# Clustered attention and gated convolution: routing by VectorE block transposes, with the order of every queue written out

## The chip, the cores and the metric

The kernel runs on one core of a Trainium2 chip. That core has TensorE (PE: matrix products and transposes by matrix product, from SBUF into PSUM), VectorE (DVE), ScalarE (ACT), GpSimd (POOL) and SyncE (SP, here only an issuer of DMAs), and 16 DMA engines. Each engine takes its own queue of instructions strictly in order; an instruction waits until the semaphores that it names have been raised. The metric is the device time of one execution in microseconds (us), lower is better. Where a time of a part is given, it comes from one profiled execution.

## The reference, cut to what matters

Two parts follow each other. The first is attention in which a query sees a key only if both fall to the same cluster, one of 16 per head:

```
B, H, S, D = 4, 8, 768, 64;  16 clusters per head
q_assign = argmax over c of  q_n . c_n        (q_n, c_n: divided by their norms; k_assign alike)
mask     = q_assign[:, :, :, None] == k_assign[:, :, None, :]
scores   = where(mask, q k^T / sqrt(D), -1e9);  attn = softmax(scores)
x        = attn v, heads side by side          -> (4, 768, 512)
```

The second is a gate around a circular convolution of length 768, done by Fourier transform:

```
x1, x2, x3 = x @ w_proj                        (512 -> 3 x 512)
y   = x1 * irfft(rfft(x2) * rfft(filter)) * x3
out = y @ w_out                                -> (4, 768, 512), fp32
```

## The kernel before

**The work.** Four batches times two groups of four heads make eight groups n = 0 to 7 (`NG`), and each group has two head pairs pr = 0, 1. For each group there is a `routing` step (L544), which prepares queries, keys and the mask, and for each pair an `attention` step (L647). After every second group, a batch's x is complete and `hyena` (L800) does projection, transform, gate and output of that batch, among the attention work of later groups; the last batch's comes after all attention.

**Attention.** For each of six key tiles of 128 keys, three score products per pair (L664) fill a PSUM bank each with 512 columns. ScalarE takes the exponential of each (L678, L681) into an SBUF tile `p`. A p-by-v block of eight matmuls (`pv`, L688, the instructions at L692) adds into two PSUM banks (4 and 5). The denominators are sums of `p` over key tiles in `acc`: the first two tiles are added in three pieces, on VectorE or GpSimd (L709), the other four by VectorE whole (L713). The sums over partitions then go by accumulating DMAs from POOL's queue (L746) and through DRAM (L750, L752), or for some groups by PE (L726).

**The mask.** It is no separate operation: 16 rows below the 64 (or above, for the second head) of the bf16 operands `aug` of the score product hold one-hot words of the cluster, 0 or 1 on the key side and -BIG or 0 on the query side, with BIG = 262144, so that a score of another cluster falls by BIG before the exponential.

**Routing, groups 1 to 7.** PE transposes queries and keys (`tr2`, L562; `tr` for group 1). Casts write the 64 rows of `aug` (L581). Then the clusters:

1. `sim` (L592, instructions at L595): 16 matmuls of 32 rows by 384 give similarities, 128 rows (query or key, pair, head, cluster) by 768 tokens, in two PSUM banks.
2. Two copies of them to SBUF by ScalarE or VectorE (L600, executed in the helper at L265 or L267).
3. `simT` (L606, at L608): six fp32 128x128 transposes on PE, into two more PSUM banks. Now 128 tokens lie on the partitions and 48 groups of 16 clusters in a row.
4. VectorE: the largest of 16 (L616, in two halves), the comparison with it (L618, two halves), a product with falling numbers BIG*16 to BIG*1 (`revx`, L621) to settle ties, four steps of maxima (`largest`, L629), and one last step on keys (is_equal) and on queries (subtract), L633.
5. One DMA transpose from SP's queue (L638) brings the words `oh` back to rows, 128 x 768 in `ohT`.
6. Eight DMAs (`masks`, L469) put 16 rows each into the `aug` tiles. A mask's 16 rows lie four apart in `ohT`.

Group 0 goes another way (`first_masks`, L474), which the change leaves as it is but for its place in the order.

**What sets the order.** Each step registers operations with `Plan.op` (L85): engines it may run on, an assumed duration, a due time, what it reads and writes, and the PSUM banks that it takes. `Plan.place` (L114) is a list scheduler that runs when the program is built. It takes at each step an engine, an operation and free banks by readiness and due time, shifted for each operation by a table `NUDGE`, with a table `ONLY` that fixes the engine for some. What it returns is the order of all queues, and the bank of every product. Loads are held back to a short time before they are due (`LEAD`).

**Shapes of PE's array.** `array` (L50) gives each PE operation the shape in which it drives the array: 32, 64 or 128 columns wide. Scores, projections and inverse transforms take the shape of the operation before them, and `product` (L70) issues them in halves of 64 or whole (L75, L73).

**VectorE and GpSimd.** Operations marked `lock` on GpSimd are made to wait for the last locked one of VectorE that stands before them in the order (L1164).

Of the kernel before, what the change touches and what calls it, by code (L numbers as in the profile page):

```python
# [35 lines left out]
LEAD = 2.99901  # L36
FIRST = 2
BUSY = 8.09741
HELD = 4
# [3 lines left out]
THIRDS = [[(0, 0, 512)], [(0, 512, 768), (1, 0, 256)], [(1, 256, 768)]]  # L43
HOLD = {"score": "score", "o": "o"}
AFTER = {"PE": .16}
OVERLAP = {"ACT": .09, "DVE": .08}
MODES = {"pv": 64, "bc": 64, "half": 64, "sim": 32, "den": 32, "score": 0, "proj": 0, "inv": 0}


# [28 lines left out]
class Plan:  # L78

    def __init__(self):
        self.ops, self.writers, self.reads = [], {}, {}

    def op(self, eng, fn, due, r=(), w=(), alloc=None, free=(), lock=False, byts=0, after=(), kind=None, lat=0.0):  # L85
        o = Op()
        o.eng = eng if isinstance(eng, dict) else {eng[0]: eng[1]}
        o.fn, o.due, o.alloc, o.free, o.lock, o.byts, o.kind = fn, due, alloc, free, lock, byts, kind
        o.seq = len(self.ops)
        o.due += NUDGE.get(o.seq, 0.0)  # L90
# [23 lines left out]
    def place(self, free0, banks_for, switch=0.1, wait=0.1, rate=215e3, bonus=10.84378, margin=0.02195, shape=1.63806):  # L114
        free = dict(free0)
        bank_free = [0.0] * 8
        ready = {e: [] for e in free}
        pend = 0
        st = SimpleNamespace(pool=0.0, dve=0.0, bw={}, last=None, kind=None, score=0, o=0, tail=0,
                             held=dict(score=0, fill=0, o=0))  # L120
# [3 lines left out]
        def enqueue(o):  # L124
# [4 lines left out]
            for e in o.eng:  # L129
                ready[e].append(o)  # L130
# [1068 lines left out]
```

## Time and profile before

| | |
|---|---|
| runs | 385.18, 386.62, 389.62 us (median 386.62) |
| span of the profiled execution, first to last instruction | 383.4 us |
| PE busy | 366.2 us, 96% |
| VectorE busy | 335.8 us, 88% |
| ScalarE busy | 258.7 us, 67% |
| GpSimd busy | 115.3 us, 30% |
| granted TensorE clock, mean | 0.997 |
| PE's first matmul | 6.27 us, held by the first load of queries |
| data moved by DMA | 47.19 MB, mean 123 GB/s |

How to read it: the profile is of one execution, and the span leaves out what lies around the first and last instruction; the median of the runs is 3.2 us above the span. A row of a group has the line of the kernel, the engine, the operation, what it writes and reads, the shape and the number of times, then the busy time in us and the mean length of one in ns, then the idle time of that engine just before, and what ended that idle time. PEld is the loading of weights, which goes beside matmuls. A row of stages has the stretch and its length, the busy time of each engine in the order PE, PEld, VectorE, ScalarE, GpSimd with the number of instructions, then the granted clock, the share of the DMA engines and GB/s. A mean over the whole span mixes a start (to 24 us), a middle and a tail (from 340 us), and each has limits of its own.

### The profile page before, as it was taken

Reading aid. Unit: us, or ns where it says so; the run is one execution under the profiler, and the core shown is the slowest. Engines: PE = TensorE matmul, PEld = TensorE weight load, DVE = VectorE, ACT = ScalarE, POOL = GpSimd, SP = SyncE. Lnnn points to the kernel's source line nnn. Section 1 sums busy time; section 2 is a strip of 40 time slices with the busy share of each in tenths; the row PEclk is TensorE's granted clock in tenths of the full one; section 3 lists DMA queues with packets and bytes.
Section 4 is the critical chain, followed back from the end, with each engine's and each line's share of the span. In section 5 each row is a group of like instructions: output and inputs, shape, how many; then the busy total and the mean of one; then the engine's idle time right before and its main releaser. Section 6 shows DMA issues by size and latency. Waiting matters only on the chain.

```text
span 383.4 us, 8667 instructions
## 1 busy us (share of the span) xinstructions
PE 366.2 (96%) x3337; PEld 223.0 (58%) x3343; DVE 335.8 (88%) x497; ACT 258.7 (67%) x483; POOL 115.3 (30%) x155
## 2 busy tenths in 40 slices
PE   3999997999999999999999999999999899999995
PEld 2555454445455564655465665667578566557883
DVE  8778797888899689988999997998998899999982
ACT  5998878787885986588784656877762458712142
POOL 8522302011014454322342443222330452212500
PEclk9999999999999999999999999999999999999998
DMA  9909967642688678466986888854666641200124
GB/s 174 237 21 208 192 151 153 149 96 78 138 164 163 111 145 143 97 114 105 194 132 163 124 166 212 131 77 77 105 97 162 146 68 9 78 11 2 55 113 164
DMA packets 93861, 47.19 MB, mean 123 GB/s; under 512 B 82088, under 2 KB 87676, under 8 KB 93820
## 3 DMA queue, kind: packets, MB, share of 16 engines
q1 hardware_dynamic: 87836, 36.84, 43.3%
q0 software_dynamic: 2704, 8.98, 16.3%
q10 hardware_dynamic: 3280, 0.82, 1.2%
q8 instruction: 26, 0.43, 0.5%
q14 instruction: 15, 0.12, 0.1%
HBM read 31.59 MB, written 7.40 MB: 102 GB/s over the span
## 4 chain that ended last, share of the span: by engine, by line
PE 73%; DVE 17%; ACT 4%; issue 3%; POOL 1%; DVEq 0%; POOLq 0%; ACTq 0%
PE bank L75 30%; PE pair L692 24%; DVE acc L713 8%; PE bank L824 6%; PE bank L564 3%; PE bank L73 2%; PE bank L595 2%; PE bank L458 2%; DVE hm L445 1%; ACT p L681 1%; PE bank L726 1%; PE bank L608 1%; PE bank L575 1%; ACT qkP L265 1%; DVE mx L616 1%
## 5 line engine op out<-in xcount | busy, mean ns | idle before, releaser
L692 PE MATMUL pair<-p,vraw 128*64 128x385 f32 x768 | 143.1, 490 | 0.3 <-ACT osb L716 0.2
L681 ACT ACTIVATE p<-bank 128x512 f32<-128x512 f32 x192 | 110.1, 609 | 26.3 <-PE bank L75 20.1
L713 DVE TENSOR_TENSOR acc<-p,acc 128x1536 f32<-128x1536 f32 x64 | 112.9, 1763 | 10.6 <-POOL acc L709 4.4
L692 PEld LDWEIGHTS pair<-p,vraw 128*64 128x64 f32 x768 | 56.1, 136 | 46.2 <-issue 39.0
L75 PE MATMUL bank<-aug,aug 128*64 128x256 bf16 (+3 forms) x652 | 70.2, 326 | 1.4 <-DVE tm L267 1.3
L678 ACT ACTIVATE p<-bank 128x512 f32<-128x512 f32 x96 | 58.0, 608 | 12.3 <-PE bank L75 12.1
L75 PEld LDWEIGHTS <-aug 80*64 80x64 bf16 (+1 forms) x652 | 40.0, 109 | 33.5 <-issue 23.0
L746 POOL DMA_DIRECT2D acc<-acc x30 | 24.2, 807 | 65.6 <-DVE acc L713 26.0
L75 PE MATMUL bank<-xT,wpj 128*64 128x384 bf16 x448 | 41.5, 326 | 0.0
L709 POOL TENSOR_TENSOR acc<-p,p 128x512 f32<-128x512 f32 x22 | 28.1, 1282 | 44.0 <-DVE acc L709 21.1
L267 POOL CAST aug<-qkP 64x768 bf16<-64x768 f32 x22 | 18.0, 821 | 68.9 <-DVE acc L713 25.7
L75 PEld LDWEIGHTS <-y 128*64 128x64 bf16 x512 | 29.8, 110 | 9.8 <-issue 4.8
L265 ACT COPY qkP<-bank 128x512 f32<-128x512 f32 (+1 forms) x47 | 23.7, 542 | 17.4 <-PE bank L75 9.4
L75 PEld LDWEIGHTS <-wpj 128*64 128x64 bf16 x448 | 28.0, 110 | 11.9 <-issue 3.8
L848 DVE TENSOR_TENSOR tm<-bank,hm 128x512 f32<-128x512 f32 x44 | 28.5, 683 | 4.8 <-POOL y L852 1.6
L852 POOL TENSOR_TENSOR y<-tm 128x512 bf16<-128x512 f32 x17 | 21.5, 1273 | 23.3 <-DVE acc L713 9.6
L265 ACT CAST aug<-qkP 64x768 bf16<-64x768 f32 x31 | 25.7, 829 | 1.7 <-DVE qkP L267 0.5
L75 PE MATMUL bank<-wout,y 128*64 128x512 bf16 x192 | 23.1, 379 | 0.0
L824 PE MATMUL bank<-wpj,xT 128*64 128x512 bf16 x192 | 22.6, 380 | 0.0
L709 DVE TENSOR_TENSOR acc<-p,p 128x512 f32<-128x512 f32 x26 | 17.7, 700 | 2.5 <-ACT p L681 1.8
L716 ACT COPY osb<-pair 128x770 f32<-128x770 f32 x16 | 12.9, 804 | 9.8 <-PE pair L692 9.6
L923 POOL TENSOR_TENSOR yy<-sd 128x384 f32<-128x384 f32 x9 | 9.0, 1003 | 33.4 <-DVE acc L713 15.1
(154 smaller groups left out, 456.9 us busy)
## 6 DMA issues: line engine op xcount, KB each, us to landing
vraw<-in_v_dram SPq DMA_DIRECT2D x16, 384.0 KB, 4.5
qkraw<-in_q_dram SPq DMA_DIRECT2D x30, 192.0 KB, 4.7
qkraw<-in_k_dram SPq DMA_DIRECT2D x30, 192.0 KB, 5.2
rb<-dr SPq DMA_DIRECT2D x30, 192.0 KB, 3.5
out_dram<-ob SPq DMA_DIRECT2D x11, 512.0 KB, 3.1
acc<-acc POOLq DMA_DIRECT2D x10, 384.0 KB, 5.6
acc<-acc POOLq DMA_DIRECT2D x10, 192.0 KB, 4.0
y<-in_moe_filter_fft_dram SPq DMA_DIRECT2D x4, 384.0 KB, 5.2
```

What stands on the lines that cost most here:

```text
L75: T.nc.tensor.matmul(out[64 * i:64 * i + 64], lhsT[:, 64 * i:64 * i + 64], rhs, start=start, stop=stop)
L265: T.nc.scalar.copy(out, in_)
L267: (T.nc.vector if e == "DVE" else T.nc.gpsimd).tensor_copy(out, in_)
L678: T.nc.scalar.activation(o, ap(h).rearrange("p (a b) -> p a b", a=2), Act.Exp, scale=0.125)
L681: T.nc.scalar.activation(flat(s)[:, lo:lo + 512], ap(h), Act.Exp, scale=0.125)
L692: T.nc.tensor.matmul(o[64 * hp:64 * hp + 64, ch, :385], T.vraw[vs][:, hp, sk * D:(sk + 1) * D], T.p[slots[sk]][:, hp, 384 * ch:384 * ch + ...
L709: alu(e).tensor_tensor(o, x, y, op=Alu.add)
L713: T.nc.vector.tensor_tensor(T.acc[os], T.p[slots[sk]][:, :, :S], T.acc[os], op=Alu.add)
L746: op(("POOL", .8), lambda e, rows=rows: T.nc.gpsimd.dma_start(flat_()[:rows], flat_()[rows:2 * rows], accum_op=Alu.add), te, r=[], w=AK, b ...
L824: T.nc.tensor.matmul(ap(h)[64 * i:64 * i + 64], T.xT[xs][:, kt, c:c + 64], T.wpj[:, kt, DM:2 * DM], start=kt == 0, stop=kt == ND - 1)
L848: op(("DVE", .68), lambda e, i=i, cs=cs, r=r, h=h: T.nc.vector.tensor_tensor(T.tm[r][:, cs], ap(h), hmrow(i, (0, 2, 2, 3)[2 * r + cs]), op ...
L852: op({"POOL": 1.5, "DVE": .68}, lambda e, i=i, r=r: alu(e).tensor_tensor(T.y[:, i, r], T.tm[r][:, 0], T.tm[r][:, 1], op=Alu.add if r else ...
```

## The change

In `routing`, for groups 1 to 7:

- The two copies of the similarities become two VectorE transposes of 32x32 blocks straight out of PSUM. A block has 32 tokens and the 32 rows of a pair's two heads, so after it tokens lie on partitions, 32 rows in each of four quadrants, and clusters in a row. `simT` and its two banks go.
- The maximum and the comparison read that SBUF tile, once over 768 in place of twice over 384 in PSUM.
- The words lie with the cluster outermost. The product with `revx` and the last step, now one subtraction for queries and keys alike, may run on VectorE or GpSimd.
- The DMA transpose becomes one VectorE block transpose of 128x768 bf16, and one more VectorE step on the key half turns the subtraction's result into 0 or 1: max with -1, then plus 1.
- A mask's 16 rows now lie next to each other in `ohT`.

`Plan.place`, `banks_for`, `NUDGE`, `ONLY` and the constants of the scheduler go. `Plan.follow` reads a string `ORDER` of 1896 words: engine letter (P, A, V, G, S), number of the operation, and for products the PSUM banks. All queues are as that string says. It keeps the rule of `array` and the dependencies.

Counted in both orders, operations that may run on several engines are shared out anew. On VectorE: 40 pieces of partial sums at L709 (26 before), 12 y sums at L852 (7), 25 folds at L923 (23), 7 casts of `aug` (11). On GpSimd: 8 pieces (22), 12 y sums (17), 7 folds (9). On ScalarE: 35 casts of `aug` (31), and more of the copies out of PSUM. PE has 612 operations, 619 before: the seven `simT` are the difference.

```diff
         for ch in range(2):
-            op(EV384, lambda e, ch=ch, h=h: copy(e, T.sim[:, ch], bank(h.ids[ch])[:, :384]), b0 + 1.4 + .1 * ch, r=[h],
-               w=[("sim", ch, 0), ("sim", ch, 1)], free=[h])
+            op(("DVE", TURN), lambda e, ch=ch, h=h: V().transpose(T.sim[:, ch], bank(h.ids[ch])[:, :384]),
+               b0 + 1.4 + .1 * ch, r=[h], w=[("sim", ch, 0), ("sim", ch, 1)], free=[h])
...
-        op(("PE", .72), simT, b0 + 2.5, r=SIM + ["ident"], w=[h], alloc=h)
...
+        op(("DVE", .87), lambda e: V().tensor_reduce(mx(), sv(), axis=AX, op=Alu.max), b0 + 2.5, r=SIM, w=both("mx"))
+        op(("DVE", .87), lambda e: V().tensor_tensor(
+            words(), sv().rearrange("p g c -> p c g"), mx().unsqueeze(1).to_broadcast([128, NC, 48]), op=Alu.is_equal),
+           b0 + 3.4, r=SIM + both("mx"), w=both("oh"), lock=True)
+        op({"DVE": .56, "POOL": 1.8}, lambda e: alu(e).tensor_tensor(
+            *[words().rearrange("p c (m i) -> p c m i", i=4)] * 2, T.revx[:].unsqueeze(2).to_broadcast([128, NC, 12, 4]),
+            op=Alu.mult), b0 + 4, r=["revx"],
...
+        op({"DVE": .56, "POOL": 1.8}, lambda e: alu(e).tensor_tensor(
+            words(), words(), T.mt[:, :48].unsqueeze(1).to_broadcast([128, NC, 48]), op=Alu.subtract),
+           b0 + 4.2, r=both("m2"), w=both("oh"), lock=True)
...
-        op(("SP", .6), lambda e: T.nc.sync.dma_start_transpose(
-            T.ohT[:].rearrange("p (t n) -> p t n", n=128), T.oh[:].rearrange("p a n c -> p (a n c)")), due - 2,
-           r=both("oh"), w=both("ohT"), byts=196e3, lat=3.0 if n < 3 else 1.0)
+        op(("DVE", .95), lambda e: V().transpose(
+            T.ohT[:].rearrange("p (b x) -> p b x", x=32).rearrange("p b (h c) -> p b h c", c=NC),
+            words().rearrange("p c (b h) -> p b h c", h=2)), due - .5, r=both("oh"), w=[("ohT", 0), ("ohT", 1)] + both("ohk"))
+        op(("DVE", .35), lambda e: V().tensor_scalar(T.ohT[64:], T.ohT[64:], -1.0, 1.0, op0=Alu.max, op1=Alu.add), due,
+           r=both("ohT"), w=both("ohk"), lock=True)
...
-    order = P.place({"PE": .3, "ACT": .8, "DVE": .8, "POOL": .8, "SP": .8}, banks_for)
+    order = P.follow(ORDER)
```

The new way of taking the order:

```python
    def follow(self, order):
        placed, last = [], None
        for word in order.split():
            name, _, banks = word.partition(":")
            o = self.ops[int(name[1:])]
            o.on = ENGINE[name[0]]
            if banks:
                o.alloc.ids = tuple(map(int, banks))
            if o.on == "PE":
                last = array(o, last)
                o.whole = last == 128
            placed.append(o)
```

More of the change, by code (lines that the diff above doesn't have):

```diff
@@ L2 @@
-import heapq
 import math
@@ L43 @@
+ENGINE = {"P": "PE", "A": "ACT", "V": "DVE", "G": "POOL", "S": "SP"}
 THIRDS = [[(0, 0, 512)], [(0, 512, 768), (1, 0, 256)], [(1, 256, 768)]]
-HOLD = {"score": "score", "o": "o"}
-AFTER = {"PE": .16}
-OVERLAP = {"ACT": .09, "DVE": .08}
+TURN = .58
 MODES = {"pv": 64, "bc": 64, "half": 64, "sim": 32, "den": 32, "score": 0, "proj": 0, "inv": 0}
@@ L112, in op @@
         return o
[L114 to L120, printed above, removed]
-        st.scores, st.otiles = (sum(o.alloc is not None and o.alloc.cls == c for o in self.ops) for c in ("score", "o"))
-        busy = dict.fromkeys(free, 0.0)
-        def enqueue(o):
-            o.ready = max([d.end - AFTER.get(d.on, 0.0) * (d in o.soft) + (0.06 if o.eng.keys().isdisjoint((d.on,)) or d.byts else 0.0)
-                           for d in o.deps] or [0.0])
-            if o.kind == "load":
-                o.ready = max(o.ready, o.due - LEAD)
-            for e in o.eng:
-                ready[e].append(o)
-        def take(o):
-            if o.alloc is None:
-                return
-            o.alloc.ids = banks_for(o.alloc, bank_free, st, o)[0]
-            for i in o.alloc.ids:
-                bank_free[i] = 1e9
-            st.score += o.alloc.cls == "score"
-            st.o += o.alloc.cls == "o"
-            st.held[HOLD.get(o.alloc.cls, "fill")] += o.alloc.n
-            if o.alloc.cls != "o":
-                st.tail |= st.o == st.otiles and any(i in (4, 5) for i in o.alloc.ids)
-        def done(o, e, t, d, end):
-            o.start, o.on = t, e
-            o.end = end + AFTER.get(e, 0.0)
-            if o.byts:
-                s, b = max(o.end + 1.3, st.bw.get(e, 0.0)), o.byts / rate
-                for f in [f for f in st.bw if f != e and st.bw[f] > s]:
-                    b += min(o.byts / rate, st.bw[f] - s)
-                    st.bw[f] += min(o.byts / rate, st.bw[f] - s)
-                st.bw[e] = s + b
-                o.end = st.bw[e] + 0.6 + o.lat
-            if e == "POOL" and o.lock:
-                st.pool = t + d
-            if e == "DVE" and o.lock:
-                st.dve = t + d
-            for h in o.free:
-                h.readers -= 1
-                h.end = max(h.end, o.end)
-                if not h.readers:
-                    st.held[HOLD.get(h.cls, "fill")] -= h.n
-                    for i in h.ids:
-                        bank_free[i] = h.end + 0.06
-            for x in o.eng:
-                ready[x].remove(o)
-            for x in o.outs:
-                x.left -= 1
-                if not x.left:
-                    enqueue(x)
-        for o in self.ops:
-            if o.seq in ONLY:
-                o.eng = {ONLY[o.seq]: o.eng[ONLY[o.seq]]}
-        for o in self.ops:
-            if not o.left:
-                enqueue(o)
-        while any(ready.values()):
-            best = None
-            for e, lst in ready.items():
-                f = free[e]
-                cand = []
-                for o in lst:
-                    t = max(f, o.ready)
-                    m = margin if e == "PE" else 0.0
-                    late = max(f, o.ready + m)
-                    if o.alloc is not None:
-                        ids = banks_for(o.alloc, bank_free, st, o)
-                        if ids is None:
-                            continue
-                        t, late = max(t, ids[1]), max(late, ids[1] + m)
-                    if o.lock and e in ("POOL", "DVE"):
-                        t = late = max(t, st.dve if e == "POOL" else st.pool)
-                    cand.append((late, o, t))
-                if not cand:
-                    continue
-                t0 = min(c[0] for c in cand)
-                c = min((c for c in cand if c[0] <= t0 + wait + 1e-9), key=lambda c: (
-                    c[1].due - (bonus if e == "PE" and st.kind == "pv" == c[1].kind else 0.0)
-                    + (shape if e == "PE" and array(c[1], st.last) != st.last else 0.0)
-                    + (BUSY if e == "DVE" and len(c[1].eng) > 1 else 0.0)
-                    + (c[0] - t0) * 20, c[1].seq))
-                if best is None or (t0, c[0]) < best[0]:
-                    best = ((t0, c[0]), e, c[1], c[2])
-            if best is None:
-                raise RuntimeError("stuck: " + repr([(e, [x.kind for x in l][:4]) for e, l in ready.items()]))
-            _, e, o, t = best
-            take(o)
-            d = o.eng[e]
-            if e == "PE":
-                mode = array(o, st.last)
-                if mode != st.last:
-                    d += switch
-                st.last, st.kind, o.whole = mode, o.kind, mode == 128
-            done(o, e, t, d, t + d)
-            busy[e] += d - OVERLAP.get(e, 0.0)
-            free[e] = t + d - OVERLAP.get(e, 0.0)
-        self.busy = busy
-        self.span = max(o.end for o in self.ops)
-        return sorted(self.ops, key=lambda o: (o.start, o.seq))
@@ L223, in banks_for @@
-def banks_for(bank, free, st, o):
-    def whole(lo, hi):
-        return max(free[lo:hi])
-    if bank.cls == "o":
-        t = whole(4, 6)
-        return ((4, 5), t) if t < 1e8 else None
-    allowed, first = [0, 1, 2, 3, 6, 7], []
-    if st.score and st.score < st.scores:
-        if st.held["score" if bank.cls == "score" else "fill"] + bank.n > HELD:
-            return None
-    if st.o == 0:
-        allowed += [4, 5] if bank.cls == "head" else []
-    elif st.o == st.otiles:
-        if st.tail:
-            allowed += [4, 5]
-        elif whole(4, 6) < 1e8:
-            first += [4, 5]
-    t = lambda i: whole(4, 6) if i in first else free[i]
-    ids = sorted((i for i in allowed + first if free[i] < 1e8), key=lambda i: (t(i), i))[:bank.n]
-    return (tuple(ids), max(map(t, ids))) if len(ids) == bank.n else None
+    def follow(self, order):
[10 more added lines that the diff above has]
+            placed.append(o)
+        assert len({o.seq for o in placed}) == len(placed) == len(self.ops)
+        return placed
@@ L303, in load_qk @@
             T.qkraw[s][:, :, hp], (T.q, T.k)[j][n // 2, 4 * (n % 2) + 2 * pr + hp].rearrange(
-                "(p t) d -> p t d", t=NT)), due, w=[("qkraw", s, hp)], byts=196e3, kind="load", after=after, lat=.5)
+                "(p t) d -> p t d", t=NT)), due, w=[("qkraw", s, hp)], byts=196e3, kind="load", after=after, lat=.5 if n else -.6)
             for hp in range(2)]
@@ L321, in centroids @@
         op(("DVE", .15), lambda e: V().tensor_scalar(cen.ss, cen.ss, 1e-30, None, op0=Alu.max), 2.3, r=["ss"], w=["ss"])
-        sq = op(("ACT", 1.5), lambda e: T.nc.scalar.activation(cen.s0, cen.ss, Act.Sqrt), 2.4, r=["ss"], w=["s0"])
+        sq = op(("ACT", 2.4), lambda e: T.nc.scalar.activation(cen.s0, cen.ss, Act.Sqrt), 2.4, r=["ss"], w=["s0"])
         def newton(e):
@@ L604, in routing @@
         both = lambda x: [(x, 0), (x, 1)]
-        def simT(e, h=h):
-            for i in range(NT):
-                T.nc.tensor.transpose(bank(h.ids[i // 3])[:, ts(i % 3, 128)], T.sim[:, i // 3, ts(i % 3, 128)],
-                                      T.ident)
-        op(("PE", .72), simT, b0 + 2.5, r=SIM + ["ident"], w=[h], alloc=h)
-        words = lambda: T.oh[:].rearrange("p a n c -> p (a n c)").rearrange("p (m c i) -> p m c i", c=NC, i=4)
-        for ch in range(2):
-            sv = lambda ch=ch, h=h: bank(h.ids[ch])[:, :384].rearrange("p (m i c) -> p m i c", i=4, c=NC)
-            mx = lambda ch=ch: T.mx[:, ch].rearrange("p (m i) -> p m i", i=4)
-            op(("DVE", .55), lambda e, sv=sv, mx=mx: V().tensor_reduce(mx(), sv(), axis=AX, op=Alu.max),
-               b0 + 3.3 + .2 * ch, r=[h], w=[("mx", ch)])
-            op(("DVE", .55), lambda e, ch=ch, sv=sv, mx=mx: V().tensor_tensor(
-                words()[:, 6 * ch:6 * ch + 6], sv().rearrange("p m i c -> p m c i"), mx().unsqueeze(2).to_broadcast([128, 6, NC, 4]),
-                op=Alu.is_equal), b0 + 3.4 + .2 * ch, r=[h, ("mx", ch)], w=[("oh", ch)], free=[h])
@@ L621, in routing @@
-        op(("DVE", .56), lambda e: V().tensor_tensor(
-            words(), words(), T.revx[:].unsqueeze(1).to_broadcast([128, 12, NC, 4]), op=Alu.mult), b0 + 4, r=["revx"],
+        sv = lambda: T.sim[:].rearrange("p a (g c) -> p (a g) c", c=NC)
+        mx = lambda: T.mx[:].rearrange("p a b -> p (a b)")
+        words = lambda: T.oh[:].rearrange("p a n c -> p (a n c)").rearrange("p (c g) -> p c g", c=NC)
+        op(("DVE", .87), lambda e: V().tensor_reduce(mx(), sv(), axis=AX, op=Alu.max), b0 + 2.5, r=SIM, w=both("mx"))
```

125 lines of the change are left out of this document (107 added, 18 removed).

## The prediction

> **What bounds the kernel now.** I read the busy table and the chain that ended last first, then the idle time of each engine by stage, then the groups of instructions that the change touches.
>
> ```profile
> PE 366.2 (96%) x3337; PEld 223.0 (58%) x3343; DVE 335.8 (88%) x497; ACT 258.7 (67%) x483; POOL 115.3 (30%) x155
> PE 73%; DVE 17%; ACT 4%; issue 3%; POOL 1%; DVEq 0%; POOLq 0%; ACTq 0%
> ```
>
> TensorE has 96% of the span and 73% of the chain; VectorE is second in both. The rest is far behind. By stage (span in us, then busy time of each engine):
>
> ```profile
> 0.00:24.00 24.00, 16.26 (x130) 11.23 (x131) 19.11 (x49) 19.26 (x39) 13.39 (x52) 1.00 0.83 166
> 24.00:340.00 316.00, 310.98 (x2730) 182.38 (x2734) 281.96 (x389) 227.71 (x422) 93.02 (x96) 1.00 0.65 127
> 340.00:383.40 43.40, 38.99 (x483) 29.36 (x479) 34.74 (x61) 11.69 (x23) 8.89 (x7) 0.98 0.19 74
> ```
>
> PE's idle 17.2 us are 7.7 in the start, 5.0 in the 316 us of the middle and 4.4 in the tail. So the middle is as long as its PE work: less PE work shortens it directly, as long as nothing else fills up. DVE has 34.0 us of idle time there (282.0 of 316, 89%). How full DVE can be kept for a while:
>
> ```profile
> 140.00:170.00 30.00, 29.95 (x257) 16.60 (x258) 28.58 (x39) 21.22 (x39) 9.46 (x10) 1.00 0.69 129
> 200.00:230.00 30.00, 30.00 (x275) 18.60 (x278) 29.00 (x38) 18.00 (x32) 11.11 (x12) 1.00 0.79 153
> ```
>
> That is 95.3% and 96.7% over 30 us, with PE still full. The groups that go, stay or change engine:
>
> ```profile
> L608 PE MATMUL bank<-ident,sim 128*128 128x128 f32 x42 | 6.1, 282 | 0.0
> L616 DVE TENSOR_REDUCE mx<-bank 128x24 f32<-128x384 f32 x14 | 7.5, 549 | 1.9 <-PE bank L608 1.9
> L618 DVE TENSOR_TENSOR oh<-bank,mx 128x384 bf16<-128x384 f32 x14 | 7.7, 555 | 0.3
> L621 DVE TENSOR_TENSOR oh<-oh,revx 128x768 bf16<-128x768 bf16 x7 | 3.9, 562 | 0.2
> L633 DVE TENSOR_TENSOR oh<-oh,mt 128x384 bf16<-128x384 bf16 x14 | 4.4, 353 | 0.1
> L709 POOL TENSOR_TENSOR acc<-p,p 128x512 f32<-128x512 f32 x22 | 28.1, 1282 | 44.0 <-DVE acc L709 21.1 <-ACT p L681 10.8 <-ACT p L678 6.9
> L709 DVE TENSOR_TENSOR acc<-p,p 128x512 f32<-128x512 f32 x26 | 17.7, 700 | 2.5 <-ACT p L681 1.8 <-issue 0.4 <-ACT p L678 0.3
> ```
>
> The path from one-hot words to masks in one round, on the DMA queue of SP (start, length):
>
> ```profile
> 79.38 1.30 SPq L638 DMA_TRANSPOSE ohT<-oh  x1
> ...
> 85.23 3.09 SPq L469 DMA_DIRECT2D aug<-ohT  x5
> ```
>
> **PE, part by part.** (1) Seven rounds lose six fp32 transposes each (simT, L608). Twelve such transposes (L564) take 1.46 us in the chain, so six take 0.73: 7 x 0.73 = 5.1 us. (2) The array of PE changes shape less often. By the kernel's own rule (`array`, L50), applied to both orders as they are written, there are 73 changes before and 54 after. A p-by-v block (L692 x8) takes 1.30 us behind work of its own shape and 1.45 behind transposes: 0.15 each, 19 x 0.15 = 2.9 us. Every other PE operation is kept, with its count. That more of the shared-shape matmuls are issued in halves costs nothing: eight halves of L75 and four wholes of L73 both stand at 0.82 to 0.88. Sum for PE: -8.0, with -5.1 as the other end if the changes of shape turn out to be hidden (by that end the time is 381.6).
>
> **DVE.** One routing round now: reductions 2 x 0.549, comparisons 2 x 0.555, product 0.562, four maxima 0.355 + 0.257 + 0.208 + 0.184 = 1.004, last step 2 x 0.353: 4.48 us; plus 4 of the 14 copies of the similarities at 0.552, so 33.6 over seven rounds. After: two turns of 128x384 out of PSUM, one reduction and one comparison of 768, the product 0.56, the maxima 1.0, one subtraction of 768 bf16 0.56, a turn of 768, and a max-and-add on 64 partitions. The trace has no turn. The nearest row of the same shape and source is the plain copy out of PSUM (L267, 128x384, 0.55); for the 768-wide ones it is L926 (128x768, 0.95). I take these, since a turn also reads and writes each element once. Lower ends are the bf16 rows, 0.35 and 0.56 (DVE then needs 290 us in the middle, and PE alone sets it); upper ends twice the copy, 1.1 and 1.9. The 768-wide reduction and comparison read fp32 from SBUF: 0.95 each (between 0.55, were width free, and 1.1, two of the old). The max-and-add: 0.35 (L633; up to 0.69, L539). Round: 1.10 + 0.95 + 0.95 + 0.56 + 1.0 + 0.56 + 0.95 + 0.35 = 6.4; seven rounds 44.9, so +11.3. The written order names DVE for the product and the subtraction in every round.
>
> That order also moves work between engines. To DVE: 14 partial sums (26 to 40) at 0.70, 5 y sums at 0.73, 2 folds at 0.55, four small copies of inv at 0.26, one qkP copy of 384 at 0.56: 9.8 + 3.6 + 1.1 + 1.0 + 0.6 = +16.1. Away from it to ACT: 4 casts of aug at 0.56, 2 copies of qkP at 0.66, 2 of tm at 0.69, 3 of x, 3 of od and 1 den at 0.55, 3 of ob at 0.69: -11.0. Together DVE gets +16.4: 335.8 becomes 352. Of this some 5 us fall behind the first score of the last head pair (the same rows give 61.0 before and 66.0 after from there to the end), where the tail has 8.7 us of idle DVE. So the middle gets 11 to 16; I take 14, 282 + 14 = 296 us.
>
> **The sum.** If the middle lost all 8.0 us it would be 308 us, with DVE at 296/308 = 96.1%: as full as its best 30 us now, for ten times as long. I give it the lower of the two stretches above, 95.5% in round numbers: 296/0.955 = 310 us. So the middle shortens by 6, not by 8. Start and tail: the same loads and the same last batch; the loads of the start share out five to ACT and three to SP, four and four before; taken as nothing, between -1 and +1 (PE's first wait for data is 6.3 us). Span 383.4 - 6.0 = 377.4. The median of the runs shown, 386.62, lies 3.2 above the profiled span; that is kept: **380.6 us**.
>
> **What costs nothing, and its cover.** ACT goes from 258.7 to about 263 (10 similarity copies of 0.479 leave, the copies above arrive) and has 88 us idle in the middle. POOL loses 14 partial sums at 1.28, 5 y sums at 1.27 and 2 folds at 1.0: 115 to 89. SP issues seven DMA transposes fewer at 1.30. Its masks for a batch's second pair now often stand behind loads; a mask lands 3.8 us (median) after its issue. What hides that is PE work: between a round's sim block and the first score that needs its masks the order puts 21 to 33 us of PE work before, 16 to 22 after (each block by its time in the chain: 0.217 a third of scores, 1.30 a p-by-v block, and so on). The path itself is shorter: from the DMA transpose at 79.38 to the first mask at 85.23 were 5.9 us, where 1.3 us of DVE stand now. If that cover is gone, PE waits up to 3.8 us a round. No PE wait of before names a mask, so I charge nothing. The two PSUM banks that simT held come free sooner, which I also count at nothing (PE waits for a bank in the middle are inside its 5.0 us).
>
> **Rivals.**
> *The port was the bound (faster still).* POOL's partial sums wait for DVE (21.1 of 44.0 us; the kernel orders such pairs itself, L1164), and DVE waits for POOL's results (4.4 us on L713, 1.6 on L848, 1.4 on L926). If DVE and POOL also exclude each other on such work, 19 operations moved away from POOL free 24 us for 13 that DVE pays, and the middle keeps all of PE's 8.0 and loses half of the 5.0 of idle: 383.4 - 10.5 + 3.2 = 376. Against it: the waits on POOL are 7.4 us in all. [...]
> *DVE eats the gain (no change).* At 93.7% in the middle, above its present 89% but below its best stretches, 296 us need 316: no gain, 386.6. For it: dips to 66% (130 to 140 us) and 74% (170 to 180) exist now, where DVE waits 2.7 us for spectrum and other banks of PE and 1.4 and 2.5 for POOL. Against it: the waits for POOL are of the kind that the new order moves away, and PE was full in both.
> *The turns are dear (slower).* At the upper ends the 21 turns cost 14.3 us more; DVE then needs 310/0.955 = 325 us, the middle grows by 9, and the time is 395.6. It decides from 302 us of DVE work on, so from turns 1.4 times my price. Against it: the dearest DVE row of 384 elements is 0.61 (L359) and of 768 is 1.04 (L792). [...]
>
> **Chances.** Forecast 0.47 (377.5 to 382.7); port rival 0.15; no change 0.23; slower, by dear turns or late masks, 0.15. A measurement of this kernel can tell about 1% from no change. So faster by over 1% (under 382.8) is 0.62, within 1% 0.23, slower 0.15. The range runs from PE's work with no idle in the middle (383.4 - 8.0 - 5.0 + 3.2 = 373.6) to short of the dear turns, 392.
>
> **What would show it.** Right: no L608 group; PE busy near 358; a turn of 384 at 0.55 and of 768 at 0.95; DVE near 352, 95% or more in the middle; POOL near 89. Wrong: turns of 0.8 and 1.4 or more; PE idle in the middle over 10 us with releasers on DVE; PE waits on masks; or PE not losing its 8 us.

## The result, and the profile after

After the change the kernel takes 387.89 us (median of 20 runs, 386.77 to 389.37), before it 385.75 (20 runs on the same chips). The ratio is 1.0059, with a 95% interval of 1.0043 to 1.0075: 0.6% slower, where 380.6 was forecast. The profiled execution took 387.75 us with a span of 386.0, so 1.8 us lie around the span.

The busy table and the chain of the kernel after, by engine:

```profile
PE 364.6 (94%) x3325; PEld 218.4 (57%) x3326; DVE 362.3 (94%) x508; ACT 263.6 (68%) x486; POOL 90.5 (23%) x134
...
PE 48%; DVE 35%; issue 6%; ACT 6%; SPq 2%; DMA 2%; POOL 1%; DVEq 0%; ACTq 0%; POOLq 0%
```

DVE gained 26.5 us of work, not 16.4, and is now as busy as PE; its share of the chain doubled from 17% to 35%, and PE's fell from 73% to 48%. The same three stages (stretch, length, then busy time of PE, PEld, DVE, ACT, POOL):

```profile
0.00:24.00 24.00, 16.19 (x123) 10.49 (x124) 20.08 (x50) 17.16 (x33) 14.06 (x53) 1.00 0.73 166
24.00:340.00 316.00, 307.46 (x2707) 178.42 (x2705) 305.10 (x397) 233.48 (x429) 70.80 (x77) 1.00 0.62 122
340.00:386.00 46.00, 40.90 (x505) 29.44 (x500) 37.13 (x63) 12.97 (x26) 5.65 (x4) 0.97 0.18 70
```

In the same 316 us DVE works 305.1 (96.6%) where it worked 282.0, and PE's idle time grew from 5.0 to 8.5. PE has also left more over: 505 of its instructions lie in the tail, where 483 did (the counts of the middle do not compare, since 42 transposes of before are gone from it). The start is unchanged; the tail is longer because work was pushed into it.

The groups that answer to the ones shown of before (DVE and POOL, one shape a row):

```profile
L605 DVE STREAM_TRANSPOSE ohT<-oh 128x768 bf16<-128x768 bf16 x7 | 14.6, 2079 | 0.1
L586 DVE TENSOR_TENSOR oh<-sim,mx 128x768 bf16<-128x768 f32 x7 | 10.9, 1559 | 0.1
L578 DVE STREAM_TRANSPOSE sim<-bank 128x384 f32<-128x384 f32 x14 | 7.5, 560 | 0.7 <-PE bank L573 0.7
L585 DVE TENSOR_REDUCE mx<-sim 128x48 f32<-128x768 f32 x7 | 6.7, 950 | 0.2
L601 DVE TENSOR_TENSOR oh<-oh,mt 128x768 bf16<-128x768 bf16 x7 | 3.9, 558 | 0.2
L608 DVE TENSOR_SCALAR ohT<-ohT 64x768 bf16<-64x768 bf16 x7 | 2.5, 357 | 0.2
...
L678 DVE TENSOR_TENSOR acc<-p,p 128x512 f32<-128x512 f32 x40 | 27.3, 702 | 1.0 <-ACT p L650 0.9
...
L678 POOL TENSOR_TENSOR acc<-p,p 128x512 f32<-128x512 f32 x8 | 10.2, 1281 | 31.3 <-DVE acc L678 8.7 <-DVE acc L682 7.2 <-ACT p L647 6.8
```

Read the means (second number after the bar) against the prices of the prediction: the turn out of PSUM, the reduction, the subtraction, the max-and-add and the partial sums stand where they were put. Two do not: the last turn is 2.08 us (0.95 taken, 1.9 the upper end) and the comparison 1.56 (0.95 taken, 1.1 the upper end). Seven rounds of 1.13 + 0.61 are 12.2 us of DVE that the sum did not have. (16.4 + 12.2 would be 28.6; the other terms together came out 2.1 us lower.)

Where PE now stands still, in stretches of 10 us of the kernel after:

```profile
90.00:100.00 10.00, 8.24 (x76) 4.06 (x74) 9.72 (x10) 7.14 (x15) 3.66 (x3) 1.00 0.57 151
...
150.00:160.00 10.00, 8.35 (x82) 5.20 (x79) 9.76 (x17) 7.30 (x15) 1.58 (x2) 1.00 0.85 147
240.00:250.00 10.00, 8.46 (x93) 5.40 (x91) 9.76 (x17) 7.04 (x14) 2.84 (x3) 1.00 0.76 133
```

PE is at 82 to 85% while DVE is at 97 to 98% (and from 40 to 50 us at 81%, with DVE at 98%). DVE is about as full in stretches where PE is full too (9.80 us of 10 from 110 us and 9.90 from 250 us, beside 10.00 of PE), so it is the waits that tie the two together. The stretch from 90 us on PE's and on DVE's timeline (start, length):

```profile
93.75 0.85 PE L695 MATMUL bank<-acc,ones 128*32 128x384 f32 x8 [1.76 <-DVE acc L682]
```

```profile
86.36 5.48 DVE L682 TENSOR_TENSOR acc<-p,acc 128x1536 f32<-128x1536 f32 x3
91.75 0.22 DVE L728 RECIPROCAL dn<-dn 128x12 f32<-128x12 f32 x1
91.94 1.76 DVE L682 TENSOR_TENSOR acc<-p,acc 128x1536 f32<-128x1536 f32 x1
```

PE stands 1.76 us for a sum. On DVE four whole sums follow each other with only a reciprocal between them, and the one that PE waits for is the last; it ends at 93.70, and PE starts at 93.75. So VectorE's queue is late, and no single operation of it waited for anything. In the stretch from 240 us the dear turn itself stands in front of what PE needs:

```profile
245.34 2.07 DVE L605 STREAM_TRANSPOSE ohT<-oh 128x768 bf16<-128x768 bf16 x1
...
247.34 0.52 DVE L882 TENSOR_TENSOR sd<-bank,od 128x384 f32<-128x384 f32 x1
...
247.91 0.62 PE L68 MATMUL bank<-aug,aug 128*64 128x512 bf16 x4 [1.54 <-DVE sd L882]
```

PE waits 1.54 us for an `sd` of L882, which starts as the turn ends. From 150 us a turn stands in the same way before an `x` of L857 for which PE waits 1.05 us. Such waits of PE's scores on L882 and L857 are 3.8 us in all in this kernel.

### The profile page after: what moved, and what is told of

The parts are those of the page before. It is cut to its first block, busy times and chain, and to the rows that moved or that the text cites. A ratio compares the mean times of both kernels' runs of the same rounds, so it can differ in the third digit from the quotient of the medians.

```text
span 386.0 us, 8603 instructions
## 1 busy us (share of the span) xinstructions
PE 364.6 (94%) x3325; PEld 218.4 (57%) x3326; DVE 362.3 (94%) x508; ACT 263.6 (68%) x486; POOL 90.5 (23%) x134
## 4 chain that ended last, share of the span: by engine, by line
PE 48%; DVE 35%; issue 6%; ACT 6%; SPq 2%; DMA 2%; POOL 1%; DVEq 0%; ACTq 0%; POOLq 0%
PE bank L68 23%; PE pair L661 14%; DVE acc L682 10%; DVE acc L678 4%; DVE ohT L605 3%; PE bank L793 3%; PE bank L542 2%; DVE oh L586 2%; ACT p L650 2%; DVE uv L806 2%; PE bank L66 2%; PE bank L435 2%; DVE x L857 1%; DVE mt L598 1%; DVE mx L585 1%
## 5 line engine op out<-in xcount | busy, mean ns | idle before, releaser
L661 PE MATMUL pair<-p,vraw 128*64 128x385 f32 x768 | 143.7, 488 | 0.2
L68 PE MATMUL bank<-aug,aug 128*64 128x512 bf16 (+3 forms) x680 | 79.9, 327 | 4.0 <-DVE x L857 2.1
L68 PEld LDWEIGHTS <-aug 128*64 128x64 bf16 (+1 forms) x680 | 41.7, 109 | 43.9 <-issue 33.2
L68 PE MATMUL bank<-xT,wpj 128*64 128x384 bf16 x464 | 46.5, 326 | 0.0
L715 POOL DMA_DIRECT2D acc<-acc x30 | 23.7, 792 | 76.8 <-DMA acc<-acc 35.1
L68 PEld LDWEIGHTS <-wpj 128*64 128x64 bf16 x464 | 32.4, 109 | 10.0 <-issue 3.8
L242 ACT CAST aug<-qkP 64x768 bf16<-64x768 f32 x35 | 28.9, 829 | 3.3 <-PE bank L68 1.6
L678 DVE TENSOR_TENSOR acc<-p,p 128x512 f32<-128x512 f32 x40 | 27.3, 702 | 1.0 <-ACT p L650 0.9
L821 POOL TENSOR_TENSOR y<-tm 128x512 bf16<-128x512 f32 x12 | 15.5, 1296 | 31.5 <-DVE tm L817 27.9
L242 ACT COPY ob<-bank 128x512 f32<-128x512 f32 x19 | 10.8, 588 | 14.5 <-PE bank L68 14.5
L542 PEld LDWEIGHTS bank<-ident,qkraw 128*128 128x128 f32 x144 | 15.5, 140 | 6.5 <-issue 1.7
L542 PE MATMUL bank<-ident,qkraw 128*128 128x128 f32 x144 | 18.7, 278 | 0.3 <-ACT p L650 0.2
```

The lines of the kernel that those rows point to most:

```text
L68: T.nc.tensor.matmul(out[64 * i:64 * i + 64], lhsT[:, 64 * i:64 * i + 64], rhs, start=start, stop=stop)
L242: T.nc.scalar.copy(out, in_)
L542: T.nc.tensor.transpose(bank(h.ids[i // 4])[:, ts(i % 4, 128)], raw(ss[i // NT], i % NT), T.ident)
L661: T.nc.tensor.matmul(o[64 * hp:64 * hp + 64, ch, :385], T.vraw[vs][:, hp, sk * D:(sk + 1) * D], T.p[slots[sk]][:, hp, 384 * ch:384 * ch + ...
L678: alu(e).tensor_tensor(o, x, y, op=Alu.add)
L715: op(("POOL", .8), lambda e, rows=rows: T.nc.gpsimd.dma_start(flat_()[:rows], flat_()[rows:2 * rows], accum_op=Alu.add), te, r=[], w=AK, b ...
```

## The experiments

Two theories at first. **VectorE is the bound:** the two steps that read with a step cost 12.2 us more than planned, and that took the gain. **PE is still the bound:** PE lost less than 8 us and the dear steps lie in cover. A third question came with the result: the order also moves sums to VectorE, and that may be what fills it. All ratios are against the kernel before, run beside it on the same chip; after itself is 1.0059, from its own 20 runs.

**The turn alone, read in order.** The words lie with the cluster outermost, so the turn's innermost read goes from cluster to cluster in steps of 48 bf16, 96 bytes. Here the same turn reads the same tile in order, so that the words land in the wrong rows; the regrouping is left out, and only the time is of use.

```diff
         op(("DVE", .95), lambda e: V().transpose(
             ...
-            words().rearrange("p c (b h) -> p b h c", h=2)), due - .5, ...
+            T.oh[:].rearrange("p a n c -> p (a n c)").rearrange("p (b h c) -> p b h c", h=2, c=NC)), due - .5, ...
```

> The 128x768 turn of the one-hot words reads its input in the order in which it lies in memory, in place of steps of 96 bytes; the words then land in the wrong rows, so the regrouping is left out and everything else is kept. Theory D (VectorE is the bound of the middle; the turn takes 2.08 us for its strided read): the turn falls to about 0.95 us, VectorE's busy time from 362 by 8 to 354, and the time by 5 to 8 us against the changed kernel, to about 381. Theory T (a 2-byte turn is slow by itself): the turn stays at 2.08 and so does the time. Theory O (the order's waits on PE, ACT and DMA set the length, not VectorE's amount of work): the turn may fall, but the time by less than 2 us.

Measured: 380.83 us (380.27 to 383.99), ratio 0.9898 [0.9855, 0.9941]. The group and the busy table of this kernel:

```profile
PE 362.8 (95%) x3325; PEld 220.8 (58%) x3326; DVE 354.7 (93%) x508; ACT 263.2 (69%) x486; POOL 90.4 (24%) x134
```

```profile
L605 DVE STREAM_TRANSPOSE ohT<-oh 128x768 bf16<-128x768 bf16 x7 | 6.8, 972 | 0.1
```

The turn is 0.97 us in order and 2.08 in steps: it is the step of the read that is dear, not the turn. 7.6 us less of DVE work made the time some 6 us shorter (0.9898/1.0059, 1.6%), which puts it inside the forecast's 377.5 to 382.7. PE's instructions are the same, so VectorE's work sets the time here for most of its length.

**The comparison with the step on the other side.** It reads similarities in order and writes words in steps of 96 bytes, in place of reading fp32 in steps of 64 bytes and writing in order.

```diff
-            words(), sv().rearrange("p g c -> p c g"), mx().unsqueeze(1).to_broadcast([128, NC, 48]), op=Alu.is_equal),
+            words().rearrange("p c g -> p g c"), sv(), mx().unsqueeze(2).to_broadcast([128, 48, NC]), op=Alu.is_equal),
```

> The comparison of 768 similarities reads them in order and writes its bf16 result in steps of 96 bytes, where it read in steps of 64 bytes and wrote in order. Same result. Theory D with a cost of strided reading alone: 1.56 falls to about 0.95, VectorE loses 4.3 us, and the time 2 to 4. If a strided write costs the same: 1.5 stays and so does the time. Theory O: the operation may fall, the time by less than 1 us.

Measured: 406.62 us (405.39 to 408.67), ratio 1.0559 [1.0516, 1.0602].

```profile
L586 DVE TENSOR_TENSOR oh<-sim,mx 128x768 bf16<-128x768 f32 x7 | 26.9, 3837 | 0.1
```

Neither alternative was near: a bf16 write in steps of 96 bytes takes 3.84 us, two and a half times the stepped read's 1.56. As a test of the bound it serves all the same: 16.0 us more of DVE work made 5.0% (1.0559/1.0059), 19 us.

**No step in either.** The words lie with the cluster innermost. Comparison and turn run in order; the maxima take their 8, 4, 2 and 1 clusters out of rows of 16, and the subtraction's broadcast lies innermost.

```diff
-        words = lambda: T.oh[:].rearrange("p a n c -> p (a n c)").rearrange("p (c g) -> p c g", c=NC)
+        words = lambda: T.oh[:].rearrange("p a n c -> p (a n c)").rearrange("p (g c) -> p g c", c=NC)
...
-            words(), sv().rearrange("p g c -> p c g"), mx().unsqueeze(1).to_broadcast([128, NC, 48]), op=Alu.is_equal),
+            words(), sv(), mx().unsqueeze(2).to_broadcast([128, 48, NC]), op=Alu.is_equal),
...
-                V().tensor_tensor(y, x[:, :n_], x[:, n_:], op=Alu.max)
+                V().tensor_tensor(y, x[:, :, :n_], x[:, :, n_:], op=Alu.max)
...
-            words(), words(), T.mt[:, :48].unsqueeze(1).to_broadcast([128, NC, 48]), op=Alu.subtract),
+            words(), words(), T.mt[:, :48].unsqueeze(2).to_broadcast([128, 48, NC]), op=Alu.subtract),
...
-            words().rearrange("p c (b h) -> p b h c", h=2)), due - .5, ...
+            words().rearrange("p (b h) c -> p b h c", h=2)), due - .5, ...
```

> The words lie with the cluster innermost, so that comparison and turn both read and write in order; the subtraction then has a broadcast innermost (0.95 in place of 0.56), and the maxima work on short rows. Same result. Theory D: comparison 0.95, turn 0.95, subtraction 0.95, so VectorE loses 9 us (362 to 353) and the time falls by 6 to 9 us, to 379 to 382, below the kernel before. Theory O: the time stays within 2 us of the changed kernel's 387.9.

Measured: 379.92 us (379.52 to 381.93), ratio 0.9878 [0.9838, 0.9917]: faster than before by 1.2% and than after by 1.8%. Its busy table with the chain, then its groups:

```profile
PE 362.0 (95%) x3325; PEld 219.9 (58%) x3326; DVE 354.8 (93%) x508; ACT 263.2 (69%) x486; POOL 90.3 (24%) x134
...
PE 61%; DVE 23%; DMA 5%; issue 5%; ACT 5%; SPq 0%; POOL 0%; DVEq 0%; ACTq 0%; POOLq 0%
```

```profile
L586 DVE TENSOR_TENSOR oh<-sim,mx 128x768 bf16<-128x768 f32 x7 | 7.3, 1038 | 0.1
L605 DVE STREAM_TRANSPOSE ohT<-oh 128x768 bf16<-128x768 bf16 x7 | 6.8, 970 | 0.1
L601 DVE TENSOR_TENSOR oh<-oh,mt 128x768 bf16<-128x768 bf16 x7 | 6.7, 958 | 0.2
```

Both dear steps come down to near the price that the prediction took (1.04 and 0.97 for 0.95), the subtraction rises from 0.56 to 0.96, and DVE has 7.5 us less. The chain goes back to PE, and the waits of PE's scores on L882 and L857 fall from 3.8 to 0.7 us. The turn alone gave as much: the intervals of the two overlap.

**What a little more work costs, on either engine, in either kernel.** Four kernels: `sim`'s first eight matmuls issued twice (the group grows from 10.5 to 15.0 us in both kernels, 4.5 us of PE), or the reduction done twice (6.7 us of DVE after, 7.7 before).

```diff
-            for ch in range(2):
+            for ch in (0, 0, 1):
```

```diff
-... lambda e: V().tensor_reduce(mx(), sv(), axis=AX, op=Alu.max), ...
+... lambda e: [V().tensor_reduce(mx(), sv(), axis=AX, op=Alu.max) for _ in range(2)], ...
```

> The changed kernel with eight of the sixteen similarity matmuls of each of seven rounds issued twice (the same values written again): 0.72 us more of PE a round, 5.0 in all. Theory D: PE has slack in the middle, the time grows by at most 1.5 us. If PE's work still sets the length: plus 4 to 5 us.

> The changed kernel with the reduction of 768 similarities done twice in each of seven rounds: 0.95 us more of VectorE a round, 6.7 in all. Theory D: plus 5 to 7 us, to 393 to 395. Theory O: plus at most 2.

> The kernel before with the same eight matmuls a round issued twice, 5.0 us more of PE. If PE's work sets the length of the kernel before, as its profile was read: plus 3 to 5 us. If not: at most 1.

> The kernel before with both reductions of 384 similarities done twice in each round: 1.1 us more of VectorE a round, 7.7 in all. If VectorE had slack in the middle (34 us idle), as its profile was read: plus at most 2 us. If VectorE already set the length at the places where it counts: plus 4 to 8 us.

Measured (cost: the ratio over the same kernel without the addition, less 1, times 386 us; in brackets with the outer ends of both intervals):

| kernel | added work | ratio over before | cost |
|---|---|---|---|
| after, more PE | 4.5 us | 1.0151 [1.0109, 1.0193] | 3.5 us [1.3, 5.8] |
| after, more DVE | 6.7 us | 1.0254 [1.0202, 1.0305] | 7.5 us [4.9, 10.1] |
| before, more PE | 4.5 us | 1.0157 [1.0061, 1.0252] | 6.1 us [2.4, 9.7] |
| before, more DVE | 7.7 us | 1.0137 [1.0068, 1.0206] | 5.3 us [2.6, 8.0] |

After the change DVE work costs about its whole length. PE work costs most of its length too, between what the two theories expected: it is no slack either, and this pair alone does not part them. Before the change PE work costs its whole length within the interval, as the prediction had it; but DVE work is not free there either, with 34 us of idle time in the middle. Some two thirds of it count, and even the lower end is 2.6 us. The intervals of before and after overlap on both engines, so this table does not show that the price of either engine's work changed.

**The sums put back.** In the written order, 27 words go from V to G and 8 from G to V, so that the partial sums and y sums run on the engines that they had before; their places in the order stay.

```diff
-... V285 ... V284 ... G349 ... V451 ...
+... G285 ... G284 ... V349 ... G451 ...
```

> The changed kernel's order, every word at its place, but the partial sums and y sums on the engine that the kernel before gave them: 27 go from VectorE to GpSimd and 8 the other way, so 14 and 5 net. Theory D (the amount of VectorE's work sets the length): VectorE loses 13 us and the time falls by 5 to 10. Theory P (VectorE and GpSimd exclude each other, and such moves free VectorE of waits): 24 us of GpSimd come back, VectorE waits for them, and the time grows by 2 to 10.

Measured: 399.72 us, ratio 1.0307 [1.0249, 1.0365], 9.5 us more than after. Its groups of partial sums, and DVE's longest wait:

```profile
L678 POOL TENSOR_TENSOR acc<-p,p 128x512 f32<-128x512 f32 x22 | 32.5, 1510 | 58.0 <-DVE acc L678 15.1 <-DVE acc L682 13.1 <-ACT p L647 7.5
L678 DVE TENSOR_TENSOR acc<-p,p 128x512 f32<-128x512 f32 x26 | 21.8, 849 | 1.5 <-ACT p L647 0.9 <-ACT p L650 0.6
```

```profile
DVE acc L682 <- POOL acc L678: 13.9, 8, 4.2
```

DVE works 6.7 us less (355.6) and the time is still longer: DVE waits 13.9 us in 8 waits for POOL's sums, waits that after does not have. Sums of the same shape also take longer on both engines at once, 849 ns for 702 and 1510 for 1281. In after, 38 of the 40 on VectorE took 648 to 700 ns each; the other two, 834 and 1316, each ran beside an operation of GpSimd, but eleven of the 38 did so too. The waits and the lengthening go in the direction of the prediction's port rival ("port" is the kernel's own word, the reason that it writes beside its locks at L1166); what causes the lengthening is not shown. But it is no clean reversal: the same shares of 26 and 22 took 700 and 1282 ns in the kernel before, whose order was made for them. How much of the 9.5 us is the place in the order is open.

The same exchange in the kernel with the cluster innermost, to see whether it is worth anything once DVE has room:

> The same exchange of engines in the kernel with the cluster innermost. Theory D: 379.9 falls by 2 to 5, until PE's work alone is left. Theory P: it grows by 2 to 10.

Measured: 392.76 us, ratio 1.0115 [1.0061, 1.0168], 9 us more than without it, with DVE at 348.9 us and 12.0 us of DVE's waits on POOL. So in this order the moved sums are not what ate the gain; an order made anew for the old shares was not run.

**Still less on DVE.** With the cluster innermost, 13 copies out of PSUM go from V to A, or only the seven of `qkP`:

```diff
-... V398 ... V396 ... V406 ... V842 ...
+... A398 ... A396 ... A406 ... A842 ...
```

> The kernel with the cluster innermost, with 13 copies out of PSUM (7 of queries and keys, 3 of x, 2 of od, 1 of ob) on ScalarE in place of VectorE, at the same place of the order: 8 us less of VectorE, 7.5 more of ScalarE. Theory D: the time falls by 2 to 4 us, to 376 to 378. If ScalarE's queue is what PE waits for at those places (exponentials stand behind the copies): it grows by 1 to 4.

> The kernel with the cluster innermost, with only the 7 copies of queries and keys moved to ScalarE: 4.7 us less of VectorE. Theory D: minus 1 to 3 us. If ScalarE is waited for: plus 0 to 3.

Measured: ratios 0.9812 [0.9764, 0.986] and 0.9812 [0.9766, 0.9858]. Both lie 0.7% (2.5 us) below 0.9878 [0.9838, 0.9917], in the direction expected of VectorE's work, but the intervals overlap. The medians, 381.43 and 380.86 us, cannot be set against 379.92: they come from another chip, where before took 387.69 and not 385.14. DVE went down to 347.1 us in the first without a gain that can be told. Which of the three is best, and whether DVE still sets the time here, stays open.

**The price of a step by itself.** The kernel with the cluster innermost, and 23 VectorE operations on 128x768 elements after its end, within each kind equal but for the distance between neighbouring elements on one side.

```diff
+    def stepped(x, k):
+        return x.rearrange("p (a c k) -> p a k c", c=16, k=k) if k > 1 else x.rearrange("p (a k c) -> p a k c", c=16, k=48)
...
+    for k in (1, 2, 4, 8, 16, 48):
+        V.transpose(flat(b16(1), k), stepped(b16(0), k))
...
+    for k in (2, 4, 16, 48):
+        V.tensor_tensor(stepped(b16(1), k), flat(f32(2), k), flat(f32(3), k), op=Alu.is_equal)
```

> The kernel with the cluster innermost, and after its last VectorE step 23 probes of 768 elements in scratch tiles, all else idle; the time of the whole is of no interest. Turns of bf16 with the input read in order and in steps of 2, 4, 8, 16 and 48 elements (4 to 96 bytes); turns of fp32 read in order and in steps of 2, 4, 16 and 48 (8 to 192 bytes); comparisons fp32 to bf16 with the first input stepped, then with the bf16 output stepped, then with an fp32 output stepped. If the step of reading is what costs: bf16 turn 0.97 in order and 2.08 at 96 bytes, fp32 turns rise likewise, comparisons 1.04 in order and 1.5 at 64 bytes. If it is 2-byte reading in particular: fp32 turns stay at 0.97 at every step. If writing 2-byte elements in steps is the dearest: 3.8 us at 96 bytes and clearly less for fp32 outputs.

Measured, each once; first the six bf16 turns, with reads in order and then at 4, 8, 16, 32 and 96 bytes (stretch, length, DVE busy; the rest is PE's clock and DMA):

```profile
373.35:374.40 1.05, 0.97 (x1) 1.00 1.01 406
374.40:375.41 1.01, 0.98 (x1) 1.00 0.90 333
375.41:376.42 1.01, 0.98 (x1) 1.00 1.00 406
376.42:377.97 1.55, 1.52 (x1) 0.76 0.13 50
377.97:379.57 1.60, 1.56 (x1) 0.50 0.00 0
...
379.57:381.66 2.09, 2.06 (x1) 0.50 0.00 0
```

then the comparison with bf16 results written at 4, 8, 32 and 96 bytes:

```profile
394.45:395.49 1.04, 1.01 (x1) 0.50 0.00 0
395.50:397.38 1.88, 1.85 (x1) 0.50 0.00 0
397.38:400.79 3.41, 3.37 (x1) 0.50 0.00 0
400.79:404.60 3.81, 3.78 (x1) 0.50 0.00 0
```

| us for 768 elements, step in bytes | in order | 4 | 8 | 16 | 32 | 64 | 96 | 192 |
|---|---|---|---|---|---|---|---|---|
| turn, bf16 read | 0.97 | 0.98 | 0.98 | 1.52 | 1.56 | | 2.06 | |
| turn, fp32 read | 0.93 | | 0.98 | 1.53 | | 1.46 | | 1.46 |
| comparison, fp32 read | 0.91 | | 0.96 | 1.51 | | 1.44 | | 1.45 |
| comparison, bf16 written | | 1.01 | 1.85 | | 3.37 | | 3.78 | |
| comparison, fp32 written | | | 1.19 | | | 1.45 | | 1.45 |

Steps of 4 and 8 bytes are nearly free in the reads, 0.96 to 0.98 for 0.91 to 0.97 in order; reads at 16, 32 and 64 bytes took 1.44 to 1.56, about half as much again, for a turn as for a comparison, and the bf16 turn 2.06 at 96. That is where the kernel's 1.56 and 2.08 come from, at 64 and 96 bytes (1.44 and 2.06 here). PE's granted clock, which reads 0.50 in most of the probes, is not what lengthens them: the comparison in order takes 0.91 under it. The bf16 write does not follow the reads: it takes 1.85 already at 8 bytes, where the bf16 read takes 0.98. Why a step costs what it does is not shown.

## Why the prediction was wrong, point by point

**The step that failed is the price of the 768-wide turn and comparison:** "I take these, since a turn also reads and writes each element once." What the count of elements leaves out is in the diff itself: `words().rearrange("p c (b h) -> p b h c")` reads bf16 96 bytes apart, and `sv().rearrange("p g c -> p c g")` reads fp32 64 bytes apart. 0.95 was 2.08 and 0.95 was 1.56. Neither upper end, 1.9 and 1.1, held. The row behind 1.9 (L926) reads in order. The row behind 1.1 (L618) does read in steps of 64 bytes, by `sv().rearrange("p m i c -> p m c i")`, but out of PSUM and in runs of four elements, and at 0.555 for 384 it was no dearer than the reduction in order beside it (0.549); so it gave no warning of the same step out of SBUF, whose price no run had shown yet.

**The rule of the sum was right, with the measured prices in it.** The prediction's 296 us of DVE work in the middle become 308 with the 12.2. At 96.6%, the measured fullness, the middle needs 319 us and the span is 383.4 + 3 = 386.4; it was 386.0. With the fullness taken from the result this is consistency and no test. (At 95.5%, as taken, it would be 390: DVE can be kept a point fuller over 316 us than I allowed.) A better test is the kernel with the cluster innermost, where turn and comparison cost 0.97 and 1.04: 0.9878 of 385.75 is 381.1, for 380.6. Part of that closeness is luck, since PE lost less than forecast there too and the 3.2 us around the span were 1.4 too many. The prediction's own deciding point, 302 us, was passed, and the rival of dear turns is what happened, though weaker than its 395.6 and for another reason: the 14 turns out of PSUM stayed at 0.56, and the turn of 768 takes 0.97 in order, so it is the 96-byte step that makes it 2.08. The port rival's 376 did not come, and no run shows a port; what the runs showed in its place are the waits and the longer sums of the sums put back.

**DVE became a bound; that it was none before is not shown.** The time that DVE is not busy (span less busy time) is 47.6 us before and 23.7 after. With the order kept and DVE's work alone changed it stays near that, 25.2 with the cluster innermost, 25.7 with the reduction doubled and 27.4 with the stepped write, while DVE's work goes from 354.8 to 377.8 us and the span from 380.0 to 405.2. But in the kernel before, the doubled reduction leaves it about where it was as well, at 49.9. So both kernels lengthen with DVE's work, and what the change took away is the room. The shares of the chain do not decide it: with the reduction doubled they are 58% for PE and 26% for DVE, where after has 48% and 35%.

**PE's 8 us.** `simT`'s 6.1 us are gone, but the page shows only 1.6 less, 364.6 and not 358. The page cannot settle it: with the same 3325 PE instructions it shows 362.0 with the cluster innermost, 364.6 after and 366.2 with the reduction doubled, at mean granted clocks of 0.998, 0.996 and 0.995. The clock makes 1.1 of these 4.2 us, as an estimate from 362.0 x 0.998/0.995 = 363.1; where the rest comes from is not shown. So this term failed too, by 4 us even with the cluster innermost. The 2.9 us of fewer changes of shape show nowhere: the p-by-v blocks, from which their price was read, take 143.1 us in all before, 143.7 after and 142.9 with the cluster innermost. What took them up is open. PE's idle time in the middle stayed at 8.5 us, under the 10 that the prediction named as a sign of being wrong.

**Right:** the turn out of PSUM (0.56 for 0.55), the reduction (0.95), product and subtraction (0.56), the max-and-add (0.36 for 0.35), POOL's 90.5 for 89, ACT's 263.6 for 263, DVE over 95% in the middle, and masks that are not late (PE's weight loads waited 1.8 us for them in all). The partial sums and y sums moved to DVE are worth their place in this order: put back, the time is longer.

**Half right:** that the bound before was PE. PE's work did count there, at 6.1 us [2.4, 9.7] for 4.5; but DVE's 34 us of idle time did not cover new DVE work, as the sum implied up to 95.5%: 5.3 of 7.7 us [2.6, 8.0] counted there too.

**The size of 3.2 us around the span** came from the median of three runs; a profiled execution has 1.8. The moves to ACT add up to 10.9 us and not 11.0, which changes nothing.

## What to carry to other kernels

Before pricing a VectorE operation from a row of the same shape, write down the distance in bytes between neighbouring elements of each operand: where it is 16 bytes or more (a turn out of SBUF took 1.52 at 16 for 0.97 in order), or 8 for bf16 results (1.85 for 1.01 at 4), take the row from an operation with that step, out of the same memory (64 bytes apart, a comparison took 0.555 for 384 out of PSUM and 1.56 for 768 out of SBUF). Where a layout must be awkward for one operation, a broadcast can be the cheaper place for it: here one subtraction at 0.96 for 0.56 bought a turn at 0.97 for 2.08 and a comparison at 1.04 for 1.56. And where two engines are each near 90%, idle time of the second is no store to draw on (here, with PE at 96% and DVE at 88%, 7.7 us more of DVE cost 5.3): double one of its operations before counting on it.

## What the runs showed of the hardware that was not expected

- A write of 768 bf16 in steps costs 1.85 us at 8 bytes, 3.37 at 32 and 3.78 at 96; of fp32, 1.19 at 8 and 1.45 at 64. Why two-byte results pay more than four-byte ones, more than twice as much in the wide steps, is open; so is why a bf16 read rises again from 1.56 at 32 bytes to 2.06 at 96, while fp32 reads take 1.44 to 1.46 from 64 to 192.
- A comparison that reads fp32 in steps of 64 bytes took 0.555 us for 384 elements out of PSUM, as little as a reduction in order (0.549), and 1.56 for 768 out of SBUF, where one in order took 1.04. The one out of PSUM read runs of four elements and the one out of SBUF runs of 48; no run parts the length of the runs from the memory.
- The same PE instructions showed a busy time of 362.0 to 366.2 us in kernels that differ in VectorE's work alone, and by the mean clocks, 0.998 and 0.995, only 1.1 us of that is clock (an estimate).
- A partial sum of 128x512 took 702 ns on VectorE and 1281 on GpSimd in one order, and 849 and 1510 in another with 22 of them on GpSimd in place of 8.
